# A gated mix of linear and softmax attention on one core: the score maxima moved forward, folded in pairs, and the attention step regrouped

## The chip, the cores and the metric

The kernel runs on one core of a Trainium2 chip. The core has five engines that work side by side and wait for each other through semaphores: TensorE (PE; its weight loads are listed apart as PEld), VectorE (DVE), ScalarE (ACT), GpSimd (POOL) and SyncE (SP), which here issues all the transfers between the device memory and the on-chip memory SBUF. Matrix products land in PSUM, eight banks of 512 fp32 values for each of 128 partitions. The metric is the device time of one execution in microseconds. Three runs of the kernel before took 1132.36, 1133.01 and 1133.53 us; the median is 1133.01.

## The reference

The input is x of 2048 tokens and 448 features, with 16 heads of 28. The output is g * A(x) + (1 - g) * B(x), g = sigmoid(x . gate_w). A is linear attention with a learned feature map, B is ordinary softmax attention. Cut to what matters:

```
def A(x):
    q, k, v = split(x @ wqkv)                     # 16 heads of 28
    phi_q = concat([softmax(q @ w_phi), softmax(-(q @ w_phi))])
    phi_k = concat([softmax(k @ w_phi), softmax(-(k @ w_phi))])
    kv = einsum("bhsf,bhsd->bhfd", phi_k, v); z = einsum("bhsf->bhf", phi_k)
    o = einsum("bhqf,bhfd->bhqd", phi_q, kv) / (einsum("bhqf,bhf->bhq", phi_q, z) + 1e-6)
    return merge(o) @ wo
def B(x):
    q, k, v = split(x @ wqkv)
    p = softmax(einsum("bhqd,bhkd->bhqk", q, k) * 28 ** -0.5)
    return merge(einsum("bhqk,bhkd->bhqd", p, v)) @ wo
```

## The kernel before

The order of the instructions on PE, DVE, ACT and POOL is the order in which the code is written; only SP's is arranged by the scheduler. A tile pool hands out a fixed number of buffers per tag, and an instruction that writes a new tile waits until the buffer's last readers are done.

Products keep fp32 accuracy by splitting an operand into a high part (a cast) and a low part (what the cast left over); a projection of 512 columns or of 448 is therefore eleven matmuls (`x3`, `run`, L98). The kernel goes through these stages:

- **Key features** (rounds t = 0 to 15, 128 tokens each): the product `pk` with the key weights folded with w_phi, the values `pva`, the maximum and the minimum over each head, two subtractions and an exponential (`features1`, L282 to L289), the sum, its reciprocal and the scaling (`features2`, on DVE and POOL), and the accumulation of kv for two rounds at a time (`kv_add`, L310).
- **Query features** (rounds q = 0 to 15 and nine more to drain): the product `pq`, the same features, transposes of them (`turn`, tile `pft`), the numerators (`numer`, tile `pn`), normalization through a transfer to device memory and back, and the output projection of A (`out_a`, tile `poa`), kept in device memory as `ga_d`.
- **Projections of B** (`proj_qk`, L394 to L401, 28 of 128 columns by 512 tokens each): they give q and k of B, high and low part, transposed, written to device memory in `q_d` and `k_d`, one array per group of four heads. Six lie among query rounds 2 to 7, the rest behind round 17. Their weights are loaded and split in rounds 0, 1, 3 and 5.
- **Values of B** (`pvb`, 16 products).
- **Attention of B**, 256 steps. Step s is one block of 128 keys for one group of four heads and one block of 512 queries; 16 steps make one such pair `gq`, 16 of them in all. A step makes the four transposed scores (`scores`, L574), exponentials of them (L577), and the values of the step before (`values`, L589), which accumulate in one PSUM bank over 16 steps. The negative of the query's maximum enters the scores through a row of the stacked operand, so the maxima of `gq` must be known before its queries are loaded, four steps ahead of its first score. Then `finish` normalizes, and the last group's steps also hold the output projections (`project_first`, `project_last`).

**The maxima.** They have a product of their own. A unit (`mx_unit`, 256 of them) takes 128 queries, 512 keys and four heads: four matmuls, each 28 rows deep, in four row strips of the array, into two PSUM tiles of two banks, and two reductions (L174 and L178). After 16 units a small reduction and a transpose (`mx_done`) give the negative maxima `nm` of one `gq`. 12 units lie among the projections, 16 among the values, and 228 in the attention steps, between the first and the second pair of scores, paced by `MX_STEPS`.

**PSUM.** Three single banks (tag `s`), one for accumulation (tag `pv`) and two tiles of two banks (tag `mx`). The units, the transposes `pft` and the numerators `pn` take the `mx` tiles. The attention steps take a single bank for each score and make one exponential of 512 columns each; once the units are done (`wide`), two scores share an `mx` tile and one exponential of 1024 columns (L579).

Of the kernel before, what the change touches and what calls it, by code (L numbers as in the profile page):

```python
# [29 lines left out]
EARLY = 6  # L30
PVN = 1
FIRST = (4, 6, 8, 10)
MX_STEPS = 231
# [7 lines left out]
def gated_mix_kernel(ctx, tc, xT, wqkB, wvB, wvA, wkAT, wqAT, phi, woA, woB,  # L41
# [14 lines left out]
    ps = ctx.enter_context(tc.tile_pool(name="ps", bufs=1, space=PSUM))  # L56
# [15 lines left out]
    q_d = scratch("qd", [GW, 2, S])  # L72
    k_d = scratch("kd", [GW, 2, S])
# [15 lines left out]
    wqA_s = front.tile([P, 2, 4, 450], F32R, tag="w3", name="wqA_s")  # L89
    wp_s = ExitStack()  # L90
    wp = wp_s.enter_context(tc.tile_pool(name="wp", bufs=1))
    wkA_s = wp.tile([P, 2, 4, 512], F32R, tag="w1", name="wkA_s")
    wvA_s = wp.tile([P, 2, 4, 512], F32R, tag="w2", name="wvA_s")
    stg = wp_s.enter_context(tc.tile_pool(name="stg", bufs=3))
# [17 lines left out]
    def stage(shape_b, n, src, nm, pool=None, tag="stg"):  # L112
        raw = (pool or stg).tile([P, 2, 512], F32, tag=tag, name=nm, bufs=2 if pool else None)
        nc.sync.dma_start(raw[:, :shape_b, :n], src)
        return raw[:, :shape_b, :n]
# [7 lines left out]
    def weight_part(w, src, n, nm, b, parts=2, low=nc.vector, **at):  # L123

        bs = slice(b, b + parts)
        raw = stage(parts, n, src[:, bs, :], f"{nm}_raw{b}", **at)
        nc.scalar.copy(w[:, 0, bs, :n], raw)
        lows.append(lambda: low.tensor_sub(w[:, 1, bs, :n], raw, f32(w[:, 0, bs, :n])))  # L128


    mxs = {"u": 0}
    nm_of = {}
    acts = []

# [4 lines left out]
    def mx_rows(tag, nm, src, c, bufs):  # L139

        r = mxp.tile([P, 512], F32R, tag=tag, name=nm, bufs=bufs)
        for j in range(4):
            nc.sync.dma_start(f32(r[32 * j:32 * j + DH]), src[DH * j:DH * j + DH, 0, c:c + 512])
        return r

    def mx_load(g):
        mxs[("kc", g)] = [mx_rows("kc", f"kc{g}_{b}", k_d[g], b * 512, 6) for b in range(4)]

    def mx_query(gq):
        g, qb = divmod(gq, NQ)  # L150
        mxs[("qc", gq)] = mx_rows("qc", f"qc{gq}", q_d[g], qb * 512, 2)

    def mx_unit():
        u = mxs["u"]
        if u >= NU:
            if u == NU:
                mx_done(NG * NQ - 1)
                mxs["u"] = u + 1
            return
        mxs["u"] = u + 1  # L160
        gq, r = divmod(u, 16)
        g, qb = divmod(gq, NQ)
        qt, kb = divmod(r, 4)
        if r == 0:
            mxs["part"] = mxp.tile([P, 16, 4], F32, tag="part", name=f"part{gq}", bufs=2)
        if r == 4 and gq + 1 < NG * NQ:
            mx_query(gq + 1)
        if r == 8 and qb == NQ - 1 and g + 1 < NG:
            mx_load(g + 1)
        qc, kc, part = mxs[("qc", gq)], mxs[("kc", g)][kb], mxs["part"]  # L170
        pm = [ps_mx(f"pm{u}_{i}") for i in range(2)]
        for j in range(4):
            js = slice(32 * j, 32 * j + DH)
            nc.tensor.matmul(pm[j // 2][:, j % 2, :], qc[js, qt * P:(qt + 1) * P], kc[js, :],  # L174
                             start=True, stop=True, tile_position=(32 * j, 0))
        p4 = part.rearrange("p (h t) k -> p h t k", t=4)
        for i in range(2):
            nc.vector.tensor_reduce(p4[:, 2 * i:2 * i + 2, qt, kb], pm[i], AX.X, ALU.max)  # L178
        if r == 15:
            red = mxp.tile([P, 16], F32, tag="red", name=f"red{gq}", bufs=2)  # L180
            nc.vector.tensor_reduce(red, part, AX.X, ALU.max)
            mxs["red"] = red
        if r == 0 and gq:
            mx_done(gq - 1)

    def mx_done(gq):

        pt = ps_s(f"pt{gq}")
# [591 lines left out]
```

## Time and profile before

One execution was profiled. Its own time was 1134.75 us and the recorded span 1133.0 us; so 1.75 us lie outside the span.

| what | value |
|---|---|
| median of three runs | 1133.01 us |
| profiled execution, its time and its span | 1134.75 us, 1133.0 us |
| ACT busy with exponentials in attention (L577, L579) | 501.9 us and 49.3 us |
| PE busy with scores L574 (narrow, wide), values L589, maxima L174 | 347.7, 30.6, 273.4, 151.3 us |
| moved by DMA | 96.58 MB, 85 GB/s on average |
| first attention scores, last values of attention | at about 356 us, at about 1120 us |

How to read the lines that follow: a group of instructions is given by its line in the kernel, its engine, its operation, the tile written and the tiles read, their shapes (partitions x elements) and the count; behind the bar stand the busy time, the mean duration in ns, and the idle time of the engine just before with the instruction that ended it. A timeline row begins with its start and its length in us. Matmuls overlap in the pipeline, so a matmul row is longer than the time until the next one starts; what a group of matmuls costs is read from start to start.

### The profile page before, as it was taken

The numbers are of one execution on the slowest core, as the hardware profiler recorded it, in microseconds if no ns is written. First come the engines' busy times: TensorE is split into PE (matmuls) and PEld (weight loads), VectorE is DVE, ScalarE is ACT, GpSimd is POOL, SyncE is SP. The second block draws the span as 40 slices with busy tenths as digits, with TensorE's granted clock in tenths as the row PEclk, the third lists the DMA queues.
The fourth block names the chain that finished last, engine by engine and source line by source line (L and its number), as shares of the span: only waits on it lengthen the run. The fifth ranks groups of instructions, "written<-read, shape, count | busy, mean of one in ns | idle before, by whom it ended". The sixth has DMA issues, their size and how long they took to land.

```text
span 1133.0 us, 16253 instructions
## 1 busy us (share of the span) xinstructions
PE 1101.1 (97%) x6360; PEld 570.8 (50%) x6360; DVE 796.7 (70%) x853; ACT 694.4 (61%) x1226; POOL 173.7 (15%) x135
## 2 busy tenths in 40 slices
PE   7998999999999999999999999999999999999997
PEld 7887788777675333333333333333333344444444
DVE  5787567326887888888888887888888877756003
ACT  4433445522124777777777777777777767666773
POOL 2344334300250000000000000000000002020300
PEclk9999899999999999999999999999999999999999
DMA  6120332256563421225231313232112512122211
GB/s 211 61 69 7 115 112 73 96 183 196 145 136 82 123 52 59 71 53 126 60 76 38 84 52 86 77 94 51 54 52 62 124 51 76 43 80 83 89 43 66
DMA packets 61957, 96.58 MB, mean 85 GB/s; under 512 B 15176, under 2 KB 23224, under 8 KB 61880
## 3 DMA queue, kind: packets, MB, share of 16 engines
q1 hardware_dynamic: 61880, 95.54, 30.5%
q8 instruction: 50, 0.82, 0.3%
q14 instruction: 27, 0.22, 0.1%
HBM read 66.56 MB, written 28.57 MB: 84 GB/s over the span
## 4 chain that ended last, share of the span: by engine, by line
PE 82%; DVE 6%; DMA 5%; ACT 3%; issue 1%; SPq 1%; POOL 0%; ACTq 0%; DVEq 0%; POOLq 0%
PE st L574 28%; PE pv L589 22%; PE pm L174 11%; PE pqk L98 3%; PE pvb L98 3%; PE pob_False L98 3%; PE sw L574 2%; DMA kd<-ev 2%; PE poa L98 2%; PE pk L98 2%; PE pva L98 2%; PE pob_True L98 1%; PE pq L98 1%; DVE part L178 1%; DMA xraw<-in_xT_dram 1%
## 5 line engine op out<-in xcount | busy, mean ns | idle before, releaser
L178 DVE TENSOR_REDUCE part<-pm 128x2 f32<-128x1024 f32 x512 | 603.0, 1220 | 141.8 <-PE pm L174 141.7
L577 ACT ACTIVATE p<-st 128x512 f32<-128x512 f32 x924 | 501.9, 596 | 173.7 <-PE st L574 168.1
L574 PE MATMUL st<-qst,kst 128*128 128x512 f32 x924 | 347.7, 451 | 2.8 <-ACT p L577 2.3
L589 PE MATMUL pv<-p,vb 128*32 128x512 f32 x2048 | 273.4, 605 | 0.0
L574 PEld LDWEIGHTS st<-qst,kst 128*128 128x128 f32 x924 | 141.6, 187 | 252.8 <-ACT p L577 231.9
L174 PE MATMUL pm<-kc,qc 28*128 28x512 f32 x1024 | 151.3, 496 | 3.8 <-DVE part L178 3.7
L174 PEld LDWEIGHTS pm<-kc,qc 28*128 28x128 f32 x1024 | 67.9, 181 | 99.0 <-DVE part L178 50.1
L260 POOL TENSOR_TENSOR oUb<-oUb,rsb 128x512 f32<-128x512 f32 x15 | 19.2, 1283 | 453.6 <-DMA rsb<-rdb 281.0
L589 PEld LDWEIGHTS pv<-p,vb 128*32 128x32 f32 x2048 | 40.5, 108 | 89.7 <-issue 88.0
L98 PE MATMUL pqk<-XH,wB 128*128 128x512 f32 x224 | 72.8, 409 | 7.5 <-POOL wB L128 5.5
L579 ACT ACTIVATE p<-sw 128x1024 f32<-128x1024 f32 x50 | 49.3, 1024 | 22.3 <-PE sw L574 22.3
L395 DVE TENSOR_TENSOR ev<-pqk,ev 128x512 fp32r<-128x512 f32 x28 | 19.3, 691 | 50.3 <-ACT ev L394 49.6
L98 PEld LDWEIGHTS pqk<-XH,wB 128*128 128x128 f32 x224 | 41.7, 191 | 20.4 <-POOL wB L128 6.6
L394 ACT CAST ev<-pqk 128x512 fp32r<-128x512 f32 x28 | 16.3, 583 | 55.0 <-PE pqk L98 31.6
L289 ACT ACTIVATE featk<-featk 128x896 f32<-128x896 f32 x16 | 15.2, 953 | 51.7 <-DVE featk L287 51.7
L289 ACT ACTIVATE featq<-featq 128x896 f32<-128x896 f32 x16 | 15.2, 953 | 49.8 <-DVE featq L287 49.8
L98 PE MATMUL poa<-woA_s,oTa 128*128 128x448 f32 x192 | 42.7, 370 | 0.6 <-POOL oTa L269 0.6
L98 PE MATMUL pk<-wkA_s,XH 128*128 128x448 f32 x128 | 38.3, 379 | 2.8 <-ACT wkA_s L234 1.2
L98 PE MATMUL pvb<-wvB_s,XH 128*128 128x448 f32 x128 | 39.2, 388 | 0.0
L98 PEld LDWEIGHTS poa<-woA_s,oTa 128*128 128x128 f32 x192 | 35.3, 188 | 6.6 <-issue 1.5
L98 PE MATMUL pq<-wqA_s,XH 128*128 128x448 f32 x128 | 38.5, 384 | 0.0
L269 POOL TENSOR_TENSOR oTb<-oUb,oTb 128x512 fp32r<-128x512 f32 x15 | 19.3, 1284 | 118.4 <-ACT oTb L268 118.4
(121 smaller groups left out, 968.3 us busy)
## 6 DMA issues: line engine op xcount, KB each, us to landing
qst<-qd SPq DMA_DIRECT2D x64, 224.0 KB
kst<-kd SPq DMA_DIRECT2D x64, 224.0 KB
od<-oTb SPq DMA_DIRECT2D x12, 512.0 KB
oL<-od SPq DMA_DIRECT2D x12, 512.0 KB
rsa<-rda SPq DMA_DIRECT2D x16, 256.0 KB
rsb<-rdb SPq DMA_DIRECT2D x15, 256.0 KB
qc<-qd SPq DMA_DIRECT2D x64, 56.0 KB
kc<-kd SPq DMA_DIRECT2D x64, 56.0 KB
```

Of the source, the lines that this page charges most:

```text
L98: nc.tensor.matmul(dst, l, r, start=i == 0, stop=i == len(todo) - 1)
L174: nc.tensor.matmul(pm[j // 2][:, j % 2, :], qc[js, qt * P:(qt + 1) * P], kc[js, :], start=True, stop=True, tile_position=(32 * j, 0))
L178: nc.vector.tensor_reduce(p4[:, 2 * i:2 * i + 2, qt, kb], pm[i], AX.X, ALU.max)
L260: (nc.gpsimd if n == 1 else nc.vector).tensor_mul(oU, oU, rs)
L269: nc.gpsimd.tensor_sub(oT[:, 1, :], oU[:, k, :], f32(oT[:, 0, :]))
L289: nc.scalar.activation(f, f, AF.Exp)
L394: nc.scalar.copy(e[:, 0, :], pq)
L395: nc.vector.tensor_sub(e[:, 1, :], pq, f32(e[:, 0, :]))
L574: nc.tensor.matmul(st, kst_of[(g, kt // 4)][:, j, (kt % 4) * P:(kt % 4 + 1) * P], qst_of[gq][:, j, :], start=True, stop=True)
L577: nc.scalar.activation(p[:, jl, :], st, AF.Exp, scale=SCALE)
L579: nc.scalar.activation(p, sts, AF.Exp, scale=SCALE)
L589: nc.tensor.matmul(pv[32 * j:32 * j + 32, :], vb[:, kt, 4 * g + j, :], pt[j // 2][:, j % 2, :], start=kt == 0, stop=kt == NT - 1, tile_pos ...
```

## The change

- **Maxima in the front.** 80 units (`NF`, the first five `gq`) are done before attention, where it were 28. For them the projections of B move to the start of the kernel: 20 of 28 before the key rounds, eight in the odd key rounds, with the weights split beside them. Two units lie in each key round, three more in rounds 3, 8 and 13, one or two in each query round, one with each of the last values.
- **The fold.** A unit of the front takes two heads and two key blocks: b against the second-to-first difference. The keys of one block are loaded as they are, those of the other block have the first subtracted on POOL (`pair_load`), so two row strips give b and two give a - b. ACT writes relu(a - b) of 1024 columns to SBUF, and two DVE instructions each add b to 512 of them and keep the maximum (`tensor_tensor_reduce`, each followed in the program by an instruction that stores it).
- **Attention steps.** Four scores in a row into two tiles of two banks, two exponentials of 1024 columns, then one visit (`mx_visit`) of three maxima into one tile of three banks with one reduction of 1536 columns, then the values of the step before. A visit that has a finished `gq` to transpose takes two maxima and the transpose. Some steps of the last group have a second visit. The output projections now take a score tile. PSUM is handed out anew for this stage (`ps2`).
- **Features.** ACT copies `pk` and `pq` from PSUM; DVE takes the extrema from the copy; POOL does the subtractions, one of the two for the first seven query rounds on DVE; the exponential is issued a round later.
- **Also moved.** q and k of B share one array in device memory, so a projection is written by one transfer; seven values of B come into the last query rounds; the split of the output weights of B goes into the attention steps.

```diff
+    def pair_load(g, c):
+        hp, b = divmod(c, 2)
+        heads = (2 * hp, 2 * hp + 1)
+        r = mx_tile("kc", f"kp{g}_{c}", 5)
+        t = mx_tile("kt", f"kt{g}_{c}", 1)
+        mx_rows(r, (0, 1), k_d[g], heads, b * 1024)
+        mx_rows(r, (2, 3), k_d[g], heads, b * 1024 + 512)
+        mx_rows(t, (2, 3), k_d[g], heads, b * 1024)
+        mxs[("kp", g, c)] = r
+        def sub():
+            for i in (2, 3):
+                js = slice(32 * i, 32 * i + DH)
+                nc.gpsimd.tensor_sub(r[js], f32(r[js]), f32(t[js]))
+        subs.append(sub)
     def mx_unit():
...
-        pm = [ps_mx(f"pm{u}_{i}") for i in range(2)]
+        pb, pd = ps_mx(f"pmb{u}"), ps_mx(f"pmd{u}")
         for j in range(4):
             js = slice(32 * j, 32 * j + DH)
-            nc.tensor.matmul(pm[j // 2][:, j % 2, :], qc[js, qt * P:(qt + 1) * P], kc[js, :],
-                             start=True, stop=True, tile_position=(32 * j, 0))
-        p4 = part.rearrange("p (h t) k -> p h t k", t=4)
-        for i in range(2):
-            nc.vector.tensor_reduce(p4[:, 2 * i:2 * i + 2, qt, kb], pm[i], AX.X, ALU.max)
+            nc.tensor.matmul((pb if j < 2 else pd)[:, j % 2, :], qc[js, qt * P:(qt + 1) * P],
+                             kc[js, :], start=True, stop=True, tile_position=(32 * j, 0))
+        rl = mxp.tile([P, 2, 512], F32, tag="rl", name=f"rl{u}", bufs=1)
+        nc.scalar.activation(rl, pd, AF.Relu)
+        col = 64 * gq + 16 * b + 4 * qt + 2 * hp
+        for i in range(2):
+            nc.vector.tensor_tensor_reduce(rl[:, i, :], pb[:, i, :], rl[:, i, :], 1.0, LOWEST,
+                                           ALU.add, ALU.max, part[:, col + i:col + i + 1])
...
+    def mx_visit():
+        pend = mxs["pend"]
+        if pend is None:
+            mx_fin()
+        f = mxs["f"]
+        n = min(3 if pend is None else 2, 4 * NU - f)
+        if n <= 0 and pend is None:
+            return
+        mxs["f"] = f + n
+        pm = ps2.tile([P, 3, 512], F32, tag="mx", name=f"pm{f}", bufs=1)
+        for i in range(n):
...
+            nc.tensor.matmul(pm[:, i, :], mxs[("qc", gq)][js, qt * P:(qt + 1) * P],
+                             mxs[("kc", g, kb)][js, :], start=True, stop=True,
+                             tile_position=(32 * j, 0))
...
+        if n:
+            nc.vector.tensor_reduce(part[:, f:f + n], pm[:, :n], AX.X, ALU.max)
...
-    def features1(pp, nm):
+    def features1(pp, nm, eng):
+        pc = bd.tile([P, H, DH], F32, tag="pc", name=f"pc{nm}", bufs=2)
+        nc.scalar.copy(pc, pp[:, :D].rearrange("p (h f) -> p h f", f=DH))
...
-        nc.scalar.activation(f, f, AF.Exp)
+        exps.append(lambda: nc.scalar.activation(f, f, AF.Exp))
...
     for i in range(2 * NT + 9):
...
+        if 1 <= t < NT:
+            mx_unit()
+        while exps:
+            exps.pop(0)()
+        if t % 2 == 0 and 0 <= t - 4 < NT:
+            kv_add(t - 4)
+            kv_add(t - 3)
         if t < NT:
             pk = ps_s(f"pk{t}")
             tok_major(pk, t, wkA_s, D)
+            fk[t] = features1(pk, f"k{t}", nc.gpsimd)
+            mx_unit()
...
+        if q >= 0:
+            mx_unit()
...
+        if q >= NT + 2 or q >= 10 and q % 2:
+            mx_unit()
...
     for s in range(NS + 16):
+        take_acts()
...
-            scores(s, 0, wide)
-        take_acts()
-        while mxs["u"] < MX0 + (s + 1) * (NU + 1 - MX0) // MX_STEPS and mxs["u"] <= NU:
-            mx_unit()
-        if s < NS:
-            scores(s, 1, wide)
+            scores(s, 0)
+            scores(s, 1)
+        mx_visit()
+        if 0 < s <= NS:
+            values(s - 1)
+            if s % NT == 0:
+                finish(s // NT - 1, s)
...
+        if s in pobs and kt in FIRST:
+            mx_visit()
```

More of the change, by code (lines that the diff above doesn't have):

```diff
@@ L162, in mx_unit @@
         g, qb = divmod(gq, NQ)
[L163 to L166, printed above, removed]
+        c, qt = divmod(r, 4)
+        hp, b = divmod(c, 2)
+        if r in (4, 9) and u // 16 + 1 < NF // 16:
+            pair_query(gq + 1, r // 9)
+        if r == 4 and gq + 1 == NF // 16:
             mx_query(gq + 1)
[L168 to L169 removed]
```

449 lines of the change are left out of this document (269 added, 180 removed).

## The prediction

> **What bounds the kernel now.** First the page, for the engines' loads and the costliest groups.
>
> ```profile
> PE 1101.1 (97%) x6360; PEld 570.8 (50%) x6360; DVE 796.7 (70%) x853; ACT 694.4 (61%) x1226; POOL 173.7 (15%) x135
> L178 DVE TENSOR_REDUCE part<-pm 128x2 f32<-128x1024 f32 x512 | 603.0, 1220 | 141.8 <-PE pm L174 141.7
> L577 ACT ACTIVATE p<-st 128x512 f32<-128x512 f32 x924 | 501.9, 596 | 173.7 <-PE st L574 168.1
> ```
>
> TensorE is the bound; VectorE's largest group (the maxima) and ScalarE's (the exponentials) both wait for it. Next the stretches of the front and of attention: window, then busy us of PE, PEld, DVE, ACT, POOL, granted clock, DMA share, GB/s.
>
> ```profile
> 8.00:12.00 4.00, 2.78 (x18) 2.41 (x17) 1.27 (x3) 2.97 (x6) 0.72 (x1) 1.00 1.03 343
> ...
> 16.00:20.00 4.00, 4.00 (x22) 3.69 (x21) 2.93 (x6) 1.14 (x2) 0.98 (x1) 1.00 0.88 273
> ...
> 11.60:99.80 88.20, 86.09 (x833) 76.70 (x834) 72.42 (x114) 34.09 (x62) 30.31 (x19) 0.98 0.25 77
> 99.80:175.60 75.80, 69.69 (x428) 56.93 (x429) 47.93 (x85) 31.70 (x43) 31.84 (x19) 0.93 0.31 89
> ...
> 357.00:922.50 565.50, 565.06 (x3146) 203.49 (x3146) 471.29 (x428) 432.61 (x810) 28.21 (x22) 1.00 0.28 70
> ...
> 113.00:116.30 3.30, 1.13 (x3) 0.33 (x1) 0.87 (x2) 0.95 (x1) 3.29 (x2) 0.50 0.27 96
> ```
>
> The last projections come before 357 us; 196 attention steps lie in 357 to 922.5, 2.885 us each, with PE busy throughout. Then the timeline of one such step, of one without maxima near the end, and of the maxima among the value projections.
>
> ```profile
> 513.76 0.73 PE L574 MATMUL st<-qst,kst 128*128 128x512 f32 x2
> ...
> 514.42 0.50 PE L174 MATMUL pm<-kc,qc 28*128 28x512 f32 x4
> ...
> 514.86 0.73 PE L574 MATMUL st<-qst,kst 128*128 128x512 f32 x2
> 514.96 2.36 DVE L178 TENSOR_REDUCE part<-pm 128x2 f32<-128x1024 f32 x2 [0.74 <-PE pm L174]
> ...
> 515.52 1.06 PE L589 MATMUL pv<-p,vb 128*32 128x512 f32 x8
> ...
> 516.51 0.50 PE L574 MATMUL st<-qst,kst 128*128 128x512 f32 x1
> ```
>
> ```profile
> 1080.08 1.19 PE L574 MATMUL sw<-qst,kst 128*128 128x512 f32 x4
> 1081.20 1.07 PE L589 MATMUL pv<-p,vb 128*32 128x512 f32 x8
> 1082.20 0.50 PE L574 MATMUL sw<-qst,kst 128*128 128x512 f32 x1
> ```
>
> ```profile
> L395 DVE TENSOR_TENSOR ev<-pqk,ev 128x512 fp32r<-128x512 f32 x28 | 19.3, 691 | 50.3 <-ACT ev L394 49.6
> ```
>
> Start to start: two scores 0.66, four maxima 0.44, two scores 0.66, values 0.99: 2.75 when nothing waits. The mean of 2.885 holds 0.13 of waits for ScalarE, which takes 4 x 0.596 a step. Four scores in a row take 1.12.
>
> **Attention after.** A step is four scores 1.12, three maxima, values 1.00. The three run in different row strips, as the four do, so I price them as 0.43 (bounds 0.35 and 0.62, the latter the longest seen, 517.18 to 517.80). Sum 2.55; bounds 2.47 and 2.74. ScalarE: two of 1.02 (L579's 1024 ns), 2.05 a step. VectorE: one reduction of 1536; from 609 ns for 448 and 1220 for 1024 elements the slope is 1.06 ns, so 1.76 us. The one maxima tile returns after 0.54 (514.42 to 514.96) + 1.76 + 0.06 = 2.36, under 2.55, so PE stays the bound. Maxima left: 1024 - 4 x 80 = 704; 11 visits take two and a transpose, so (704 - 22)/3 + 11, about 239 visits; nine of them are second visits in a step, so 230 steps hold maxima. 230 x 2.55 = 586; 26 steps without, at 2.26 (the buffer's return: 0.83 from score to exponential, two exponentials 1.99, less 0.56 of scores), 59. Output projections as now: 16 x 2.02 + 12 x 0.71 = 41. They now take a score buffer: 0.2 x 28 = 6; second visits 4. Together 696, against 760 now (357 to 1117.4). The last step's chain stays 15.6 (1117.4 to 1133).
>
> **The fold by itself.** A front unit has four matmuls (0.45), a Relu over 1024 on ScalarE (1.02, by L240's 1010 ns) and two VectorE passes, each followed by a small instruction that stores the maximum. Nearest row for a pass: L395, 691 ns. Bounds for the store: 0 and 175 ns (L325, the smallest VectorE instruction). Two reductions back to back take 2.36, not 2 x 1.22, so an instruction hides some of its start behind the one before: I take 0.06, so 2 x 0.75 = 1.50 a unit, bounds 1.38 and 1.73. No row shows this operation, so the rows bound it only if it runs like a plain two-source pass (rival A is the other case). It is 1.50 of VectorE for what takes 2.36 now, but it serializes. The built program's waits show that a unit's second tile waits for the unit before's two passes: 0.25 + 0.15 + 1.02 + 0.05 + 1.50 = 2.97 at least from unit to unit, and PE must find that much other work.
>
> [...]
>
> **The front after**, in its order. *Projections first.* Start 13 (before: first matmul at 4.4, first projection at 11.6; now input and weights come first), 19 units at 2.77 (the chain of waits has pqk pieces of eleven matmuls at 2.76) 52.6, four folds 1.8: 67. DMA beside it: 20 writes of 512 KB, x 4.2 MB, weights 3.9, keys 1.1: 19.7 MB; 343 GB/s at share 1.03 and 273 at 0.88 say some 310 at most, 64 us. Both full at once: 72, bounds 67 and 80. *Wait for the first pair keys*: the write of a projection that is done 5.5 us before the key rounds start has to land (writes of this size take 4 to 8 in the chain of waits), be read back (2 to 4) and be subtracted on POOL (2 x 1.28, after L260), 9 to 14 in all, beside 5.5 + 2.3 of PE work: 4, bounds 0 and 8. The SP queue issues those 20 small loads ahead of the last two key writes, and POOL's feature subtractions stand behind the key ones; both catch up within the first rounds, since nothing reads key features before round 4. PE would stand idle there; at 113.00 the clock is at 0.50 in such a gap.
>
> *Key features*, 16 rounds: pk 2.26, pva 2.26, two units 0.9, half a projection 1.39, kv 0.48: 7.3. Every other gap between units is only 2.71 wide: once 2.97 is needed (0.26), once 3.2, since the copy of pk (0.53) delays the Relu and the extrema (1.1) the passes (0.5). So 7.3 + 0.38 = 7.68; x 16 = 123, three extra units with 2.2 of wait 8, folds 1.6, less 2.4 for the first rounds: 130. Bounds 120 (all hidden) and 145.
>
> *Query features*, 25 rounds. The transposes (pft), the numerators (pn) and the units share the same two PSUM tiles, and each takes the one that was released first. Rounds 0 to 2 are bound by VectorE (extrema 1.1, a subtraction 0.61, sums 1.41, passes 1.5), 4.7 each with the waits between: 14. Rounds 3 to 8 go in pairs. In one round the next pft waits for the passes: pft 0.79, pq 2.26, drain 0.15, copy 0.53, extrema 1.1, subtraction 0.61 (to round 6), sums 1.41, passes 1.5, three hand-overs 0.15: 8.5. In the other it waits for the Relu alone: 0.79 + 2.26 + 0.45 + 1.02 + 0.33 = 4.85. That is 13.3 a pair, 12.8 for the last: 39.5. Round 9, with poa 2.47, is full: 7. Rounds 10 to 15 hold a third unit per pair, whose second tile waits for the second one's passes: 7.9 for the even round (pft, pq, unit, poa 2.47, pn 1.88), then 7.95 to the passes' end and 1.5 to the Relu's: 17.35 a pair against 14.8 of PE work, 52. Rounds 16 to 18, by the same steps without pq: 21; 19 to 24, two units of 2.97 each: 35.7. Together 169; PE work alone 138; upper bound 190. *Nine values* with a unit: 2.97 each, 27 (now 2.91: 313.76 to 316.67 and so on).
>
> What this front sheds: 99.8 to 175.6 holds nine query rounds and six projections, 9 x 4.0 + 6 x 2.77 = 53 of PE work in 75.8; with the weights split ahead of the rounds those waits go (rounds 0 to 8 take 53.5 above, their share of projections 17 elsewhere). The feature subtractions leave VectorE for POOL, at 1.14 each (L614) beside 1.70: 4.0 of a 7.7 round, hidden. If not hidden, exp would be late, and kv three rounds on.
>
> **Sum.** 72 + 4 + 130 + 169 + 27 = 402 for the front, now 357: 45 lost, as 52 more units move here. Attention 696: 64 won. 402 + 696 + 15.6 = 1113.6; the profiled run of before is 1134.75 with a span of 1133.0, so 1.75 more: **1115**. The profiled run lies 1.7 above the median of 1133.01; that is not corrected. Less than 0.2%, 2.3 us, could not be told from no change.
>
> **Rivals.** *A (slower): the fold's chain.* A pass with its store at 1.03 instead of 0.75 puts 0.56 on each of some 70 exposed units: +39, 1154. It decides from 0.26 a unit on, that is 0.88 a pass (18 us over 70). For it: no row has the operation, and before 357 us VectorE is already 82% busy in the key rounds. Against: 691 ns for the like. *B (slower): the step's weight loads show.* If three maxima cost 0.62 and the values' loads no longer overlap, the step is 2.74, as now without waits: +44, 1159; even at 2.63. For it: the 0.62 occurs; against: most are 0.43. *C (faster): the front is hidden.* PE work alone: 67 + 120 + 138 + 27 = 352, 50 less: 1065. For it: the key rounds of before run with PE 98% busy. Against: two tiles per unit out of two. *D: the projections stay DMA-bound* at 250 GB/s: 79 instead of 72, 1122, still faster.
>
> **Chances.** The forecast (with D) 0.44, A 0.22, B 0.13, C 0.16, several small losses that cancel the gain 0.05. Range: from half-way to C with some speed in attention, 1072, to B, 1160; the forecast's own is 1095 to 1132. Faster: the forecast and C, 0.60; same 0.05; slower, A and B, 0.35.
>
> **What would show it.** Attention spanning 670 to 720 us with PE full and two 1024-wide exponentials per step; the reduction of three banks at 1.76; a pass near 0.69; PE idle in the query rounds released by ScalarE and VectorE; the first unit late by some 4. Wrong if a pass is above 0.9, if the step is above 2.63, or if the front ends past 420.

## The result

The changed kernel takes 1161.39 us (median of 4 runs, 1160.19 to 1162.2) against 1133.27 us for the kernel before on the same chip (4 runs): the ratio is 1.0248, 95% interval 1.023 to 1.0265. It is 28 us slower, where 1115 us, 18 us faster, was forecast. The profiled execution took 1162.2 us, with a span of 1160.4 us and a mean granted clock of 0.976; before it was 0.991.

The same parts of the page of the changed kernel first: the engines, then the exponentials, the reduction over three banks, and the two halves of a front unit, the fold on VectorE and the Relu on ScalarE.

```profile
PE 1092.5 (94%) x6360; PEld 591.2 (51%) x6360; DVE 689.0 (59%) x841; ACT 743.6 (64%) x876; POOL 248.6 (21%) x211
...
L756 ACT ACTIVATE p<-st 128x1024 f32<-128x1024 f32 x512 | 497.6, 1021 | 160.8 <-PE st L754 159.2
L287 DVE TENSOR_REDUCE part<-pm 128x3 f32<-128x1536 f32 (+1 forms) x239 | 413.3, 1729 | 200.9 <-PE pm L276 179.9
...
L248 DVE CUSTOM_DVE_ANT_0 rl<-pmb,rl 128x512 f32<-128x512 f32 x160 | 103.2, 682 | 76.4 <-ACT rl L245 76.1
...
L245 ACT ACTIVATE rl<-pmd 128x1024 f32<-128x1024 f32 x80 | 82.2, 1028 | 36.2 <-PE pmd L242 32.9
```

The operations cost what was forecast: 1021 ns an exponential, 682 ns a fold pass (0.69 was taken), 239 visits (239 were counted). TensorE's share has fallen from 97 to 94%: it waits more. Where, the stretches of the span show (window, then busy us of PE, PEld, DVE, ACT, POOL, granted clock, DMA share, GB/s). They are the projections, the key rounds, query rounds 0 to 8, 9, 10 to 15, 16 to 18, 19 to 24, the nine values, the stretch from the last value to the first scores, the first 10 us of attention, its next 502 us, and the rest up to the last scores, most of it the last group.

```profile
13.00:66.50 53.50, 53.50 (x241) 43.14 (x241) 29.50 (x35) 23.17 (x35) 5.01 (x11) 1.00 0.85 288
70.00:207.00 137.00, 130.39 (x1046) 100.88 (x1047) 89.80 (x212) 71.53 (x111) 64.69 (x55) 0.96 0.21 65
206.90:262.40 55.50, 41.82 (x304) 31.16 (x301) 45.99 (x91) 32.81 (x41) 25.02 (x20) 0.97 0.12 35
262.40:272.70 10.30, 8.21 (x35) 6.58 (x36) 4.61 (x8) 4.12 (x5) 6.21 (x6) 0.83 0.33 90
272.70:334.00 61.30, 51.42 (x272) 38.66 (x270) 30.53 (x69) 33.68 (x45) 34.96 (x28) 0.94 0.19 58
334.00:365.90 31.90, 28.41 (x125) 19.51 (x125) 12.59 (x32) 14.63 (x18) 12.80 (x12) 0.75 0.25 79
365.90:402.70 36.80, 36.75 (x189) 28.38 (x189) 18.45 (x54) 20.84 (x29) 14.17 (x12) 1.00 0.25 81
402.70:429.00 26.30, 26.30 (x134) 20.26 (x132) 10.56 (x34) 13.52 (x18) 16.85 (x10) 1.00 0.77 164
429.00:432.90 3.90, 1.89 (x10) 0.82 (x9) 1.37 (x6) 1.56 (x2) 0.00 (x0) 0.90 0.94 185
432.90:443.00 10.10, 9.50 (x31) 4.44 (x29) 4.50 (x7) 5.70 (x7) 0.00 (x0) 0.53 0.56 124
443.00:945.00 502.00, 499.92 (x2922) 198.39 (x2919) 348.21 (x227) 386.02 (x414) 32.82 (x26) 1.00 0.31 78
945.00:1144.80 199.80, 187.16 (x1009) 87.87 (x1013) 81.92 (x59) 128.55 (x144) 33.01 (x28) 1.00 0.21 67
```

Against the terms of the sum:

| term | forecast, us | measured, us |
|---|---|---|
| projections, to the first key round | 72 | 66.5 |
| wait for the first pair keys | 4 | 3.5 |
| 16 key rounds | 130 | 136.9 |
| query rounds 0 to 2 | 14 | 13.5 |
| query rounds 3 to 8 | 39.5 | 42.0 |
| query round 9 | 7 | 10.4 |
| query rounds 10 to 15 | 52 | 61.3 |
| query rounds 16 to 18 | 21 | 31.9 |
| query rounds 19 to 24 | 35.7 | 36.8 |
| nine values | 27 | 26.3 |
| from the last value to the first scores | 0 | 3.9 |
| attention | 696 | 711.9 |
| tail | 15.6 | 15.6 |

The query rounds are 195.9 us together, against 169. (The expectations below put their end one value product earlier and call them 193.5.) The first scores start at 432.9 us, before at 355.8: 77.1 more. From there to the end of the last scores it is 711.9 us against 761.6: 49.7 less. That is the 27.4 us between the two spans. The largest miss is in query rounds 9 to 18, 23.6 us, and it begins with the round in which the low parts of `oTa` are first made. The chain of waits in rounds 11 and 12 (start, length, what; the whole loop comes back 21 us later):

```profile
280.98 2.49 POOL oTa L365 x2
...
283.49 0.78 ACT oUa L336
...
290.47 0.52 PE pmd L242 x2
...
291.06 1.03 ACT rl L245
...
292.14 1.96 PE pft L451 x8
294.09 2.97 PE pq L104 x11
...
298.35 0.95 POOL featq L382
299.30 0.90 POOL featq L384
...
300.32 1.70 POOL featq L395
302.02 1.23 POOL oTa L365
```

GpSimd makes the low parts; only then may ScalarE copy the next numerators into the buffer (`oUa`, L336), since there are two. Behind that copy stand ScalarE's other copies, behind them the features, and GpSimd takes the two subtractions (L382, L384), the scaling (L395) and the next low parts in this order. The transposes and the product of that round are slow as well: `pft` 1.96 us at a granted clock of 0.50 (292.1 to 294.1 us) where it takes 1.06 at 1.00 (at 226.95 us), `pq` 2.97 for 2.26. The view of the tile `oUa` gives sums (us, times). The first line is idle time ahead of the tile's own instructions that the low parts ended; the second is the wait of the copy into the tile:

```profile
  POOL oTa L365: 18.0, 4
...
  ACT oUa L336: 22.4, 5
```

In the kernel before, the copy waited 1.6 us in one place.

### The profile page after: what moved, and what is told of

The parts are those of the page before. It is cut to its first block, busy times and chain, and to the rows that moved or that the text cites. A ratio compares the mean times of both kernels' runs of the same rounds, so it can differ in the third digit from the quotient of the medians.

```text
span 1160.4 us, 16421 instructions
## 1 busy us (share of the span) xinstructions
PE 1092.5 (94%) x6360; PEld 591.2 (51%) x6360; DVE 689.0 (59%) x841; ACT 743.6 (64%) x876; POOL 248.6 (21%) x211
## 4 chain that ended last, share of the span: by engine, by line
PE 81%; DVE 6%; ACT 5%; POOL 3%; issue 3%; DMA 1%; SPq 1%; ACTq 0%; POOLq 0%; DVEq 0%
PE st L754 22%; PE pv L766 21%; PE pm L276 9%; PE pqk L104 6%; PE pva L104 3%; PE pk L104 3%; PE pvb L104 3%; PE pob_False L104 3%; DVE part L287 2%; PE pmb L242 2%; PE poa L104 2%; PE pq L104 2%; POOL oTa L365 1%; PE pob_True L104 1%; ACT rl L245 1%
## 5 line engine op out<-in xcount | busy, mean ns | idle before, releaser
L756 ACT ACTIVATE p<-st 128x1024 f32<-128x1024 f32 x512 | 497.6, 1021 | 160.8 <-PE st L754 159.2
L287 DVE TENSOR_REDUCE part<-pm 128x3 f32<-128x1536 f32 (+1 forms) x239 | 413.3, 1729 | 200.9 <-PE pm L276 179.9
L754 PE MATMUL st<-qst,kst 128*128 128x512 f32 x1024 | 312.7, 424 | 6.0 <-DVE acc L783 2.6
L754 PEld LDWEIGHTS st<-qst,kst 128*128 128x128 f32 x1024 | 173.0, 189 | 231.1 <-ACT p L756 183.8
L248 DVE CUSTOM_DVE_ANT_0 rl<-pmb,rl 128x512 f32<-128x512 f32 x160 | 103.2, 682 | 76.4 <-ACT rl L245 76.1
L276 PE MATMUL pm<-kc,qc 28*128 28x512 f32 x704 | 120.8, 497 | 9.3 <-DVE part L287 8.7
L245 ACT ACTIVATE rl<-pmd 128x1024 f32<-128x1024 f32 x80 | 82.2, 1028 | 36.2 <-PE pmd L242 32.9
L276 PEld LDWEIGHTS pm<-kc,qc 28*128 28x128 f32 x704 | 45.0, 182 | 97.8 <-DVE part L287 86.9
L242 PE MATMUL pmd<-kp,qp 28*128 28x512 f32 x160 | 42.2, 517 | 14.1 <-DVE part L248 8.3
L242 PE MATMUL pmb<-kp,qp 28*128 28x512 f32 x160 | 40.8, 505 | 6.7 <-ACT rl L245 3.5
```

Source lines behind the costliest of these rows:

```text
L242: nc.tensor.matmul((pb if j < 2 else pd)[:, j % 2, :], qc[js, qt * P:(qt + 1) * P], kc[js, :], start=True, stop=True, tile_position=(32 * ...
L245: nc.scalar.activation(rl, pd, AF.Relu)
L248: nc.vector.tensor_tensor_reduce(rl[:, i, :], pb[:, i, :], rl[:, i, :], 1.0, LOWEST, ALU.add, ALU.max, part[:, col + i:col + i + 1])
L276: nc.tensor.matmul(pm[:, i, :], mxs[("qc", gq)][js, qt * P:(qt + 1) * P], mxs[("kc", g, kb)][js, :], start=True, stop=True, tile_position= ...
L287: nc.vector.tensor_reduce(part[:, f:f + n], pm[:, :n], AX.X, ALU.max)
L754: nc.tensor.matmul(st[:, jl, :], kst_of[(g, kt // 4)][:, j, (kt % 4) * P:(kt % 4 + 1) * P], qst_of[gq][:, j, :], start=True, stop=True)
```

## Experiments

Four theories. **Q**: GpSimd's queue and the two `oUa` buffers. **U**: the units, their chain from products to folds and back. **T**: a unit or any other work costs its TensorE time and no more. **C**: the granted clock, which is halved behind gaps (0.53 from 432.9 to 443.0 us), so that a gap costs more than itself. Ratios are to the kernel before.

**The feature subtractions back to VectorE.**

```diff
-            fq[q] = features1(pq, f"q{q}", nc.vector if q < 7 else nc.gpsimd)
+            fq[q] = features1(pq, f"q{q}", nc.vector, nc.vector)  # both subtractions
```

> Both subtractions of every query round go back to VectorE; everything else is as in the changed kernel (1161.4 us). Theory Q (GpSimd's queue: the subtractions stand ahead of the scaling and of the low parts of oTa, and ScalarE's copy of the numerators waits for those): GpSimd loses 1.85 us a round, the wait of the oUa copy for oTa (18.0 us in 4 in the changed kernel) falls below 6 us, a pair of query rounds falls from 20.9 to 17 to 19 us and the kernel to 1138 to 1150 us. Theory U (the units themselves, their folds and the shared PSUM buffers set the rounds): VectorE, which runs the folds, gets more work, a pair of rounds stays at 20.9 us or grows, and the time is 1160 to 1170 us.

Measured 1166.69 us, 1.0303 (1.0283 to 1.0322): slower still. The time lies in the range of U, but what grew is the wait that Q names: that of the copies, to 29.7 us in 6. GpSimd's timeline (start, length, ..., idle before and its end) says why:

```profile
302.76 1.70 POOL L395 TENSOR_TENSOR featq<-featq,fsumq 128x896 f32<-128x896 f32 x1 [9.39 <-DVE fsumq L394]
304.41 2.52 POOL L365 TENSOR_TENSOR oTa<-oUa,oTa 128x512 fp32r<-128x512 f32 x2
```

The scaling now waits for VectorE's sums, and the low parts wait behind the scaling. So the work moved to GpSimd is not what makes the loop; it is what the low parts stand behind, whoever is late.

**A third buffer; the low parts on VectorE; their old place in the order.**

```diff
-        oU = pool.tile([P, n, 512], F32, tag="oU", name=f"oU{nm}", bufs=2)
+        oU = pool.tile([P, n, 512], F32, tag="oU", name=f"oU{nm}", bufs=1 + n)
```

> The numerators' copies get a third buffer, nothing else changes. Theory Q in its narrow form (only the reuse of two buffers ties ScalarE to GpSimd's queue): the oUa copy no longer waits for oTa, ScalarE runs ahead, and the time falls by 8 to 20 us to 1141 to 1153 us. Theory Q in its wide form (GpSimd's queue is late itself, by its own work): the wait moves to the output products or the scaling, and the time falls by less than 4 us. Theory U: within 2 us of 1161.4.

```diff
-            nc.gpsimd.tensor_sub(oT[:, 1, :], oU[:, k, :], f32(oT[:, 0, :]))
+            (nc.vector if n == 2 else nc.gpsimd).tensor_sub(oT[:, 1, :], oU[:, k, :], f32(oT[:, 0, :]))
```

> The two low parts of oTa in each pair of rounds (1.27 us each) go from GpSimd to VectorE; the feature subtractions stay on GpSimd. Theory Q: GpSimd loses 2.5 us a pair of rounds and the copy of the numerators waits for VectorE in place of it, whose queue is shorter: a pair of rounds falls to 17 to 19 us, the time by 8 to 20 us. Theory U: VectorE gets 2.5 us more a pair, ahead of the folds, and the time stays or rises by up to 5 us.

```diff
             turn(y - 2)
+        if y >= 7 and y % 2 and tb - 3 < 8:
+            oTs[tb - 3] = normalize4(ta, num.pop(tb - 3), f"a{tb - 3}", 2)
...
-        if y >= 7 and y % 2 and tb - 3 < 8:
-            oTs[tb - 3] = normalize4(ta, num.pop(tb - 3), f"a{tb - 3}", 2)
```

> Order alone: in each odd query round the casts and low parts of oTa are issued at the start of the round, ahead of the round's feature subtractions and of the scaling, as the kernel before does it; two buffers, nothing else changed. Theory O (the place in GpSimd's in-order queue: behind the subtractions and above all behind the scaling, which waits for VectorE's reciprocal, the low parts release the buffer late, and ScalarE's copy of the numerators waits for it): the oUa copies' wait for oTa (22.4 us in 5) falls below 5 us, and the time falls by 9 to 17 us, as much as with a third buffer (1147.4), to 1144 to 1152. Rival B (two buffers are too few in any order, since in this round the copy comes before the release): the wait stays above 15 us and the time is 1158 to 1163.

The third buffer gives 1147.36 us, 1.0132 (1.0098 to 1.0166), and the copies' wait is 1.9 us; VectorE for the low parts 1151.66, 1.0163 (1.0135 to 1.019), and the copies no longer wait for them. The order alone gives 1158.61, 1.0216 (1.0169 to 1.0264), not told apart from the changed kernel. The copies no longer wait for the low parts there, so neither theory's sign came whole: the low parts themselves wait at the head of GpSimd's queue for ScalarE's casts, with the features behind them (waiting line and what for: us in total, times, longest):

```profile
POOL oTa L365 <- ACT oTa L364: 36.3, 7, 12.9
```

So theory Q holds in its narrow form, for 10 to 14 of the 28 us: the release of a buffer must not hang on an in-order queue which itself hangs on ScalarE. Theory O, order alone, falls.

**Units left out.** In `mx_unit` the products, Relu and folds stand under a condition, which is false in the query rounds (first run) or everywhere (second run).

```diff
-    def mx_unit():
+    def mx_unit(work=True):
...
+        if work:
             pb, pd = ps_mx(f"pmb{u}"), ps_mx(f"pmd{u}")
...
-            mx_unit()
+            mx_unit(False)
```

> Left out: the score products, the Relu and the folds of the units of the query rounds (their loads and all bookkeeping stay, and their maxima are zero), that is 28 units up to the values. Theory U: the stretch of query rounds (193.5 us in the changed kernel) falls by far more than the units' 28 x 0.86 us = 24 us of TensorE, to 145 us or less. Theory Q: TensorE and VectorE lose that work, but GpSimd's loop in rounds 10 to 15 stays as long (18 to 21 us a pair), and the stretch falls by 10 to 25 us only, to 168 to 184 us.

> Left out: score products, Relu and folds of all 80 front units (loads and bookkeeping stay, maxima are zero); oUa has three buffers, so it stands against the run with three buffers alone (1147.4 us, first scores at 418.9 us of its span). Theory T (a unit costs its TensorE time, 4 products, about 0.86 us): the first scores come at 418.9 - 80 x 0.86 = 350 us or a little later. Theory U (folds, the Relu and the shared PSUM buffers cost more than the products): they come at 310 to 338 us, 1.0 to 1.35 us a unit. Either way the run shows what the front takes with none of the added work.

Without the units of the query rounds 1130.3 us, 0.9973 (0.9958 to 0.9989). These are 36 units, not the 28 of the expectation. The query rounds fall by 27 us, from 195.9 to 168.5, or 0.76 a unit; rounds 10 to 15 still take 51.9 us, and the copies' wait for the low parts has grown to 33.3 us in 6. The loop does not need the units. Without any unit, beside the run with three buffers, the first scores come at 349.5 us in place of 418.9 us: 69.4 us for 80 units, 0.87 each.

The expectations take some 0.86 us for the four products alone, but the timeline of the run with three buffers shows that they take half of it. First a unit that waits for nothing, up to the product behind it, then one that waits:

```profile
280.49 0.51 PE L242 MATMUL pmb<-kp,qp 28*128 28x512 f32 x2
280.50 0.50 PE L242 MATMUL pmd<-kp,qp 28*128 28x512 f32 x2
280.93 2.71 PE L104 MATMUL poa<-woA_s,oTa 128*128 128x448 f32 x12
283.57 0.50 PE L242 MATMUL pmb<-kp,qp 28*128 28x512 f32 x2
284.91 0.50 PE L242 MATMUL pmd<-kp,qp 28*128 28x512 f32 x2 [0.84 <-DVE part L248]
286.58 1.88 PE L451 MATMUL pft<-ident,featq 128*112 128x128 f32 x8 [1.17 <-ACT rl L245]
```

Start to start the first takes 0.44 us, as the prediction priced it (0.45), and the second 3.01. At 0.44 the products of 80 units are 35 of the 69.4 us, an estimate. Much of the rest is waiting: in this run TensorE waits 9.4, 7.1, 3.5 and 3.5 us in the four longest waits for Relu and folds. So a unit costs about twice its products, and theory T does not hold for the units. Nor is the 1.0 us a unit or more of U reached.

**The units' order.**

```diff
-        pb, pd = ps_mx(f"pmb{u}"), ps_mx(f"pmd{u}")
-        for j in range(4):
+        pd, pb = ps_mx(f"pmd{u}"), ps_mx(f"pmb{u}")
+        for j in (2, 3, 0, 1):
```

> Order alone, in the changed kernel with its two oUa buffers and one Relu buffer: a unit issues the two products that the Relu reads (pmd) ahead of the two that only the folds read (pmb), and takes the PSUM tiles in that order. Theory U (the chain from unit to unit, folds -> pmd 0.5 -> Relu 1.03 -> folds 1.3, about 3 us, is what the rounds with two units and the drain at the end wait for): pmd now waits for the Relu before (early) and pmb for the folds, the chain falls to Relu 1.03 + folds 1.3 = 2.4 us since the one Relu buffer still ties them, and the time falls by 5 to 15 us below 1161.4, to 1146 to 1156. Theory Q (GpSimd's queue and the oUa buffers are the whole loss): within 3 us of 1161.4.

The second run adds the third `oUa` buffer and, from query round 2 on, a second Relu buffer (`kvT` takes a buffer of `ga` to make room):

```diff
-        rl = mxp.tile([P, 2, 512], F32, tag="rl", name=f"rl{u}", bufs=1)
+        rl = rl_pool[u % len(rl_pool)].tile([P, 2, 512], F32, tag="rl", name=f"rl{u}", bufs=1)
...
+            rl_pool.append(ta)
```

> As relu_half_first, with three oUa buffers and, from the third query round to the values, a second Relu buffer, which lets the Relu run beside the folds of the unit before: the unit chain falls to about 1.7 us in the query rounds. If both theories hold and add up (the buffers 14 us, the chain 8 to 18), 1130 to 1140 us, level with the kernel before; if only the buffers count, 1145 to 1150.

Products for the Relu first: 1150.59 us, 1.0153 (1.0121 to 1.0184), 11 us won by order alone, though the copies still wait 21.8 us in 5 for the low parts. With three buffers and the second Relu buffer 1136.86, 1.003 (1.001 to 1.0049): the two add up (14.0 and 10.8 us make 24.8, measured 24.5); what the second Relu buffer does in it was not tried alone. So a part of U does hold: the chain from unit to unit delayed TensorE's work beside it.

A second change of order did not help, the unit at the start of the query round:

```diff
-        if 1 <= t < NT:
+        if 1 <= t < NT or q >= 0:
             mx_unit()
...
-        if q >= 0:
-            mx_unit()
```

> With three oUa buffers the unit of each query round is issued at the start of the round (as the key rounds do with one of theirs) in place of behind the feature sums. Theory U (the fold waits in VectorE's order behind the extrema, sums and reciprocals, and the PSUM buffers that the transposes need come free late: PE pft <- ACT rl 9.4 us, pmd <- part 3.7, pn <- rl 3.5 in the run with three buffers alone): these waits shrink, and the time falls by 6 to 15 us below 1147.4. Theory T (only TensorE's time counts): within 3 us of 1147.4. Against it: the early Relu delays the exponential of the features, so a loss of up to 5 us is possible as well.

1151.76 us, 1.0156 (1.0135 to 1.0177) against 1.0132 (1.0098 to 1.0166): nothing won, and 4.4 us more than three buffers alone, with intervals that overlap.

**The drain, and the clock.** First the last units as second units of earlier value rounds:

```diff
         mx_unit()
+        if t in (8, 10, 12):
+            mx_unit()
```

> With three oUa buffers the last units are issued as second units of three earlier value rounds, so that none is left to be done alone between the values and the first scores. In the changed kernel the first scores begin at 432.85 us, the last value product at 428.7: 4.2 us, and the first step takes 3 us more than a later one. Expected: the values round-trip grows by one unit's 0.9 us at most, the gap shrinks to 0.5 us, and the time falls by 3 to 6 us below 1147.4. Rival: the gap is the wait for the loads of the stacks or the switch of the PSUM pools, and the time stays within 1.5 us.

> As relu_half_first_three_buffers, with the last units issued as second units of three earlier value rounds. With the old order of products this cost 12 us in the value rounds (348.7 to 426.5 us against 349.7 to 415.0), since a second unit waited for the first one's folds and the clock was halved after the gap. Theory U: with the short chain the doubles cost their 0.9 us each, the drain (4 us) goes, and the time is 3 to 5 us below relu_half_first_three_buffers. Rival: the doubles still leave gaps and a halved clock, and it is 3 to 10 us above it.

1153.47 us, 1.0173 (1.0144 to 1.0203), 6 us more than three buffers alone, though the intervals overlap. The timeline of PE around one second unit (its first products at 395.04) shows the chain, and then the clock: pairs of matmuls of `pvb` that take 0.67 and 0.57 us in the product before take 1.11 and 0.95, at a granted clock of 0.51 (396.8 to 400.2 us).

```profile
393.24 0.49 PE L242 MATMUL pmb<-kp,qp 28*128 28x512 f32 x2
393.37 0.50 PE L242 MATMUL pmd<-kp,qp 28*128 28x512 f32 x2
395.04 0.57 PE L242 MATMUL pmb<-kp,qp 28*128 28x512 f32 x2 [1.16 <-ACT rl L245]
396.38 0.52 PE L242 MATMUL pmd<-kp,qp 28*128 28x512 f32 x2 [0.78 <-DVE part L248]
396.83 1.11 PE L104 MATMUL pvb<-wvB_s,XH 128*128 128x448 f32 x2
...
398.12 0.95 PE L104 MATMUL pvb<-wvB_s,XH 128*128 128x448 f32 x2
```

With the units' new order it gives 1140.54, 1.0057 (1.0037 to 1.0076), 3.7 us above the version without it, again with intervals that overlap. The second time that is the rival; the first time neither the forecast nor its rival came. Nothing is won by moving the last units. Next, the same place with TensorE kept busy by products that nothing reads:

```diff
+    warm(8)                 # 8 matmuls of 448 columns into a PSUM tile without a reader
     while mxs["u"] < NF:
         mx_unit()
+        warm(8)
```

> The changed kernel with 16 products added that nothing reads (448 columns, 0.206 us each, 3.3 us of TensorE), in the two gaps of the drain between the last value and the first scores, where TensorE stands idle for some 3 us. Theory C (a gap costs more than itself: the granted clock is at a half for about 10 us behind it, 432 to 442 us, 5 us lost): the clock stays at 1.00 there, the added products hide in the gaps, and the time falls by 3 to 6 us below 1161.4. Rival: the halved clock there has another cause, or costs nothing, and the time is 1161 to 1165.

The start of attention in the changed kernel, three windows, and then in this run, one window:

```profile
432.00:435.00 3.00, 2.80 (x6) 1.45 (x6) 1.00 (x5) 1.92 (x2) 0.00 (x0) 0.51 0.81 157
435.00:438.50 3.50, 2.97 (x9) 1.73 (x9) 2.34 (x4) 2.04 (x4) 0.00 (x0) 0.50 0.23 60
438.50:442.00 3.50, 3.50 (x13) 1.08 (x14) 1.23 (x1) 1.16 (x3) 0.00 (x0) 0.50 0.69 165
```

```profile
429.20:439.20 10.00, 9.59 (x53) 3.81 (x52) 6.47 (x9) 7.17 (x9) 0.00 (x0) 1.00 0.70 157
```

The clock stays at 1.00, and from the first scores to the last the stretch takes 707.5 us, where it took 711.5. The median is 1158.62 us, 1.0221 (1.0198 to 1.0243): 2.8 us less, though the interval overlaps that of the changed kernel, and just short of the 3 to 6 us of theory C. The same in the query rounds:

```diff
+        if 9 <= q < 18:
+            warm(4, f"keep{q}")
```

> The changed kernel with four products that nothing reads (448 columns, 0.83 us together at full clock) added at the end of each of the query rounds 9 to 17, just ahead of the transposes that wait there: 9 x 0.83 = 7.5 us more work for TensorE. Theory C (the halved clock is a cause: 15 us of TensorE's speed are lost between 207 and 363 us, and the slowed transposes and products, 1.96 for 1.06 and 2.97 for 2.26, lie in the loop of waits): the added work fills gaps, the clock rises from 0.92 to 0.97 or more in 260 to 340 us, and the time falls by 2 to 8 us below 1161.4. Rival T (the clock only follows the gaps, and work added is work added): the time rises by 3 to 8 us. Within 2 us of 1161.4: the added work hides, but the clock is not kept by so little.

1158.65 us, 1.0231 (1.0218 to 1.0244): with 7.5 us more work for TensorE the time does not rise; it is 2.7 us lower, again with intervals that overlap. The clock did not rise to 0.97 between 260 and 340 us, as theory C had it: it is 0.91 there, and 0.89 in the changed kernel. Behind that it is better, as the same two windows of the changed kernel and of this run show:

```profile
323.00:343.00 20.00, 16.29 (x65) 11.69 (x65) 9.45 (x21) 10.13 (x13) 11.86 (x10) 0.75 0.21 64
343.00:362.00 19.00, 16.62 (x86) 11.08 (x82) 5.51 (x15) 8.21 (x11) 7.77 (x8) 0.81 0.27 85
```

```profile
323.00:343.00 20.00, 17.89 (x90) 13.32 (x90) 9.36 (x21) 10.02 (x13) 11.56 (x10) 0.91 0.20 63
343.00:362.00 19.00, 16.26 (x90) 11.25 (x88) 6.68 (x18) 10.14 (x12) 8.18 (x8) 1.00 0.28 92
```

So the work in these gaps was free and bought some clock back. At the start of attention theory C is shown by the windows and by the 4 us of the stretch; what it is worth in the whole time lies within the noise, 2.8 and 2.7 us, and it is not the main cause. In the trace of the changed kernel one stretch at about half clock lasts 3.4 us (292.0 to 295.4, 0.52), another about three times that (432.0 to 442.0, 0.50).

**All together.** `relu_half_first_three_buffers` with the busy drain, then with the busy query rounds too, then with the first unit behind the first value product, which is also tried alone.

```diff
             fk[t] = features1(pk, f"k{t}", nc.gpsimd)
-            mx_unit()
+            if t:
+                mx_unit()
...
             value_a(t)
+            if t == 0:
+                mx_unit()
```

> relu_half_first_three_buffers (1136.9) with the 16 unread products in the drain before attention, which brought 2.8 us in the changed kernel. If the pieces add up, 1132 to 1135 us, level with the kernel before (1133); if the shorter unit chain has already closed the drain's gap, 1136 to 1139.

> combined_drain_busy with the four unread products at the end of query rounds 9 to 17 too. Theory C: there is little left to win there, since the clock in 260 to 340 us is 0.91 to 1.00 already; between -3 and +4 us against combined_drain_busy. Rival T: +5 to +8 us.

> Order alone, in the changed kernel: the first unit, which waits 3.5 us for GpSimd's key differences while TensorE stands idle, is issued behind the first value product (pva) in place of ahead of it. The 2.3 us of that product fill the wait, and the halved clock behind it (0.77 in 72.6 to 80 us, 1.7 us lost) may go: 2 to 4 us less than 1161.4, 1157 to 1160. Rival: the next unit then waits for this one's folds and the gain is given back within the first rounds: 1160 to 1162.

> combined_drain_busy (1132.9, ratio to the kernel before 1.0009) with the first unit behind the first value product. If the gain of 2 to 4 us adds up, 1129 to 1131 us, the first version below the kernel before; if it is given back, 1132 to 1134.

The first gives 1132.85 us, 1.0009 (0.9995 to 1.0022), level with the kernel before: the changes together win back the 28 us. The 4 us that the busy drain adds to them are again within overlapping intervals. Its query rounds 0 to 8, 9, 10 to 15 and the stretch to the first value:

```profile
207.80:261.30 53.50, 41.96 (x306) 31.03 (x300) 45.57 (x89) 33.34 (x42) 24.47 (x20) 0.97 0.12 35
261.30:267.50 6.20, 6.20 (x35) 5.28 (x36) 4.30 (x7) 3.33 (x4) 6.03 (x5) 1.00 0.52 139
267.50:316.90 49.40, 46.80 (x273) 35.46 (x271) 32.63 (x71) 34.28 (x45) 34.74 (x28) 1.00 0.24 75
316.90:342.30 25.40, 21.64 (x129) 14.88 (x127) 13.29 (x32) 14.29 (x18) 13.69 (x12) 1.00 0.26 85
```

Rounds 9 to 15 take 55.6 us where 59 were forecast and 71.7 had been measured. With busy query rounds it is 1139.0, 1.0059 (1.0045 to 1.0073): where the gaps are closed and the clock is whole (1.00 from 261.3 us on, above), most of the added work is paid, 6 of 7.5 us. The first unit late brings nothing, alone (1160.4, 1.0239, 1.0222 to 1.0255) or in the sum (1134.64, 1.0015, 0.9998 to 1.0031); alone, TensorE then waits for the Relu and folds of that unit instead. No version beats the kernel before.

**The gain side.** Products and reductions of the visits are left out.

```diff
-            nc.tensor.matmul(pm[:, i, :], mxs[("qc", gq)][js, qt * P:(qt + 1) * P], ...
...
-            nc.vector.tensor_reduce(part[:, f:f + n], pm[:, :n], AX.X, ALU.max)
```

> Left out: the score products and the reductions of all attention visits (704 scores; loads and the transposes of the group maxima stay). It prices the gain side. If a step is the sum of TensorE's pieces, as predicted (scores 1.12, maxima 0.43, values 1.00), steps of 2.59 us fall to 2.1 to 2.3 us, the attention stretch (432.9 to 1144.4) from 711.5 to 580 to 620 us and the time to 1030 to 1070. If the exponentials of 1.02 us a pair with their hand-overs set the step whatever TensorE does, it falls by less than 40 us.

1076.81 us, 0.9506 (0.9492 to 0.952). From first to last scores 624.8 us in place of 711.5: a visit costs 86.7 / 239 = 0.36 us, 0.12 a product. That is just outside the forecast, which priced a visit's three products at 0.43. A product in the front costs 0.87 / 4 = 0.22 with its waits, and 0.44 / 4 = 0.11 where it waits for nothing.

## Why the prediction was wrong

- **The step that failed** is "Query features, 25 rounds", 169 us against 195.9, and in it "Rounds 10 to 15 hold a third unit per pair ...: 17.35 a pair" with the clause "The feature subtractions leave VectorE for POOL ...: 4.0 of a 7.7 round, hidden". The rounds were worked out from the two shared PSUM tiles and the work between them, without the `oUa` buffers. GpSimd was counted by its load, and its load does fit (35.0 of 61.3 us). What it holds up was not followed: the low parts of `oTa` behind the scaling, the `oUa` buffer behind the low parts, and all of ScalarE's queue behind the copy into that buffer. In the chain a pair takes 21 us. A third buffer, which unties the copy from the low parts, takes 14 us off the kernel. Of the 46 us between 1115 and 1161, the query rounds are 27, attention is 16, and all other terms together 4.
- **The clock was no term of the sum.** The prediction showed a stretch with 0.93 and a gap with 0.50, and then priced every TensorE piece at full clock. From 206.9 to 365.9 us the windows lose 0.03 x 55.5 + 0.17 x 10.3 + 0.06 x 61.3 + 0.25 x 31.9 = 15 us of TensorE's speed, an upper bound for what it costs there, since part of it falls in waits. Rounds 3 to 8, with waits but almost the full clock (0.97 from 206.9 to 262.4 us), were forecast well (42.0 for 39.5).
- **The unit chain** of "2.97 at least from unit to unit" is 3.02 in the trace (the products `pmd` start at 429.11 and at 432.13 us), and was rightly named as the price of the fold. That the sum fits is in part luck: the two passes with their stores take 1.31 us, where 1.50 was forecast and 1.38 was the lower bound, and the products ahead of the Relu take 0.50, where 0.25 was. That it hangs on which half of a unit is issued first was not seen; turning them round wins 11 us.
- **Attention**, 696 against 711.9. The step was right: 2.55 forecast, 2.56 the median of the steps in the trace, and 2.25 the median of the first 192 steps of the run without visits (2.26 forecast). The first 192 steps take 499 us in place of 192 x 2.55 = 490; the halved clock at their start (5 us) and longer steps at the ends of groups, up to 2.9 us, lie in that. The other 6 us are in the last group with its output projections, and were not taken apart.
- **Other terms.** The drain of 3.9 us was forecast as nothing: the last units run alone, in their chain. Projections were 5.5 us better than forecast, since the loads did not bind as assumed. The key rounds took 6.9 more, with 7.1 us of waits for folds, Relu and keys between 60 and 206 us and a clock of 0.96; that was not taken apart further.
- **Rivals.** A, a slow fold, is refuted: a pass takes 682 ns and at most 0.62 us with its store until the next one starts, where A needed 0.88. B, a slow step, is refuted by 2.56. C, a hidden front, is refuted: the first scores come at 432.9 us, where PE work alone would be 352, and 80 units cost 69 us, twice their products. D is refuted by the 66.5 us. The loss came from none of them; that the time lies near B's 1159 is chance.
- **The trade itself.** The change takes 52 units, 208 products, out of attention and puts them into the front. A product costs about the same in both if it waits for nothing: 0.11 us in the front, 0.12 in attention. By the two runs that leave work out, some 52 x 0.87 = 45 us are paid for 208 x 0.12 = 25 us saved, an estimate from the means; of the 45 us only 52 x 0.44 = 23 are products. The other half of what attention gained is left for the regrouped steps, which were not tried alone. What a front without the waits of the units would bring stays open: the combined version comes out even and still waits 6.8, 5.2, 2.4 and 1.9 us for Relu and folds.

## What to carry to other kernels

When work is moved to an engine that is mostly idle, do not ask whether it has room; ask what its in-order queue releases late, and follow each buffer from its last reader to its next writer and on to what stands behind that writer. Price a gap on TensorE with the halved clock behind it (here 3.4 to 10 us at 0.52 and 0.50), and look at the order of products inside a unit: the half that feeds the longest chain goes first. A matmul moved from one TensorE-bound stage to another cost about the same here, 0.11 and 0.12 us; what decided was the waiting that came with it. So price a moved product with its waits in both stages, and compare that with its price when it waits for nothing.

## What was not expected of the hardware

- The clock halved without a long gap. Between 429.0 and 432.9 us TensorE waited 1.17 and 0.84 us, with products between, and was busy for 1.89 of 3.90 us; then it ran 10 us at 0.50 although busy for 9.27 of them (432.0 to 442.0 us). Some 3 us of unread products in these gaps kept it at 1.00 (429.2 to 439.2 us in `drain_kept_busy`).
- The clock differs between executions of one kernel and goes with the time. In ten runs of `relu_half_first_three_buffers` it lies between 0.983 and 0.990 and the time between 1140.9 and 1131.8 us, about 1.2 us for each 0.001. One thousandth of the span is 1.1 us, so the clock could account for most of this kernel's spread. That is not a rule for all: in the runs of the kernel before beside the last experiments, 17 on each of two chips, the slope is 0.3 and 0.5 us for each 0.001. Whether the clock sets the time there, or longer gaps lower the clock, is not shown.
- A two-source VectorE pass with a running maximum, one source in PSUM, takes 682 ns for 512 columns, and the instruction behind it that stores the maximum 83 ns; from the start of a pass to the start of the next it is 0.55 to 0.62 us.
